# Second feed-forward layer of a fused attention and two-layer kernel: token operands spread over five pairs of chunks, swish reordered, six output buffers, right-hand pools shifted by 96 bytes

## The chip, the cores and the metric

The kernel runs on one core of a Trainium2 chip as one program. The metric is the device time of one execution in microseconds (us). One execution was also profiled; its span runs from the first to the last instruction. PE is the matmul engine (TensorE), PEld its weight loads, DVE is VectorE, ACT is ScalarE, SP issues the DMAs. Nothing runs on the host.

## The reference

Windowed attention, a gated feed-forward layer (512 to 1536 to 512) and a second feed-forward layer (512 to 2048 to 512) over 2304 tokens, all in float32. The change sits in the second layer; its arithmetic is

```python
def _moe2_ref(x, w_in, w_out):          # x 2304x512, w_in 512x2048, w_out 2048x512
    h = x @ w_in
    relu6 = np.clip(h + 3.0, 0.0, 6.0)
    g = h * relu6 / 6.0                 # called swish below
    return (g @ w_out).astype(np.float32)

def reference(**kwargs):
    ...
    attn_out = _attn_ref(**attn_kwargs)
    x = np.ascontiguousarray(attn_out.transpose(0, 2, 1, 3)).reshape(B * S, H * D)
    x = _moe_ref(x=x, **moe_kwargs)     # silu(x @ w_gate) * (x @ w_val) @ w_out
    return _moe2_ref(x=x, **moe2_kwargs)
```

## The kernel before

**Number format.** Every float32 operand of a layer matmul is split into a rounded part (hi, a cast on ACT) and the rest (lo, a subtraction on DVE). A product of two operands is three matmuls: hi by hi, lo by hi, hi by lo. So each operand costs one ACT cast and one DVE subtraction.

**First layer.** Five blocks of tokens (four of 512, one of 256) by twelve chunks of 128 hidden columns. Per chunk there are 36 matmuls: gate and value (L398 to L400, twelve each) and the way back (L451 to L453, twelve). Each chunk has three weight tiles, 36 in all. The weights are stationary operands here. They lie in two pools: `wp` on the left (`RING` = 18 buffers: tiles 0 to 16 and 35) and `wq` on the right (tiles 17 to 34, that is chunks 6 to 11 apart from the very last tile, and the way back of chunk 5). Right-hand pools are stacked downwards from the end of the memory. In the built program the tiles of `wp` start at byte 10,880 + 4096 k, a multiple of 64, and those of `wq` at 155,616 + 4096 k, 32 more than a multiple of 64. The other right-hand pools (`cv`: weights being converted; `at`: attention) have the same odd 32. Attention and the conversion of the weights run beside the first four blocks. In the last block, as chunks of `wp` fall free, it becomes a ring for the weights of the second layer.

**Second layer.** Three stages of 768 tokens, two halves of 384 each (`TH`). The hidden columns are taken as eight pairs of chunks per stage, so 24 passes of `unit`, plus one that only finishes the last. The first product of the layer is computed as a 2 by 2 block product with seven products in place of eight. Its token side needs seven operands per stage: `x11`, `x21`, `x22` and the sums `t1` to `t4`. Function `operands` makes them: 7 casts (L481), 7 subtractions for lo (L483) and 4 for the sums (L488), each 128x768. It is a generator; `advance` takes steps from it. Stage 0's operands are made during the last block of the first layer. Those of stages 1 and 2 are made during passes 5 and 6 of the stage before, six steps in the middle and six at the end of a pass.

A pass issues on PE, in this order: product `x11` (1), product `t2` (2), way back of block 11 of the pass before (9 matmuls), products `x21` (3) and `t3` (4), way back 22, products `t1` (5) and `t4` (6), way back 21, product `x22` (7), way back 12. A product is 6 matmuls of 384 columns (L518 to L520), a way back 9 of 512 (L557 to L559). Products write to two PSUM banks, `g` and `v`, in turn, so each waits until the product two before it was read: 3 waits for the copy `q1` on ACT (L582), 4 for `u2`, 5 for `h11`, 6 for `u3`, 7 for `h22` and `u4`, the next pass's 1 for `h21` and its 2 for `h12` (all L576 on DVE). The swish of a block is `swish_a` (L528, L529 on DVE and the cast `gh`, L533, on ACT) and `swish_b` (`gl`, L539 on DVE). Blocks 21 and 12 get their swish in the pass after. The tile that holds `h21` shares its buffer with the `gh` of the same block of the pass before (one tag), and so does `h12`: `h21` waits for way back 21 to have read it and `h12` for way back 12.

The order on each engine is as written from block 2 of the first layer on (`manual_schedule`); before that a scheduler sets it. All DMAs are issued on SP's queue in the order written. Pass 24 has only the four ways back; each of the last two leaves three result banks, which ACT scales into one of two buffers (L562) and SP stores (L564).

Of the kernel before, what the change touches and what calls it, by code (L numbers as in the profile page):

```python
# [21 lines left out]
NT = B * S  # L22
# [13 lines left out]
NU = NC2 // 2  # L36
RING = 3 * NC1 // 2
GB = 4
# [18 lines left out]
def attention_two_ffn(ctx: ExitStack, tc, qk, v, w, out):  # L57
# [3 lines left out]
    xp = ctx.enter_context(tc.tile_pool(name="xp", bufs=1))  # L61
    wp = ctx.enter_context(tc.tile_pool(name="wp", bufs=RING))
    early = ExitStack()
    wq = early.enter_context(tc.tile_pool(name="wq", bufs=3 * NC1 - RING, side="right"))
# [128 lines left out]
    def load_x2(s, k, j):  # L193

        t = ring_tile(("x", s, k, j), [128, 2, TH], F32, "xb")
        t0 = (2 * s + j) * TH
        lo = t0
        while lo < t0 + TH:
            tb = lo // TB
            hi = min(t0 + TH, tb * TB + SIZE[tb])  # L200
            nc.sync.dma_start(
                out=t[:, :, lo - t0:hi - t0],
                in_=x2_d[tb][:, 2 * k:2 * k + 2, lo - tb * TB:hi - tb * TB],
            )
            lo = hi
        x_raw[s, k, j] = t

    def load_ring():

        while ring_free() and (x_wanted or w_next[0] < NS * 6 * NU):  # L210
            if x_wanted:
                load_x2(*x_wanted.pop(0))
                continue
# [261 lines left out]
    def operands(s, pool):  # L475


        def split(name, t):
            hi = pool.tile([128, 2, TH], F32R, tag=f"h{name}", name="xh")
            lo = pool.tile([128, 2, TH], F32R, tag=f"l{name}", name="xl")  # L480
            nc.scalar.copy(hi, t)  # L481
            yield
            nc.vector.tensor_tensor(out=lo, in0=t, in1=hi.bitcast(F32), op=ALU.subtract)  # L483
            yield
            xops[s, name] = (hi, lo)

        def minus(out, a, b):
            nc.vector.tensor_tensor(out=out, in0=a, in1=b, op=ALU.subtract)  # L488

        x11, x12, x21, x22 = (x_raw.pop((s, k, j)) for k in range(2) for j in range(2))  # L490
        yield from split("x11", x11)
        minus(x11, x12, x11)
        yield
        yield from split("t1", x11)
        minus(x11, x22, x11)
        yield
        yield from split("t2", x11)
        yield from split("x21", x21)
        minus(x12, x22, x12)
        yield  # L500
        yield from split("t3", x12)
        minus(x21, x21, x11)
        yield
        yield from split("t4", x21)
        yield from split("x22", x22)
        for k in range(2):
            for j in range(2):
                read.add(("x", s, k, j))

# [32 lines left out]
    def ffn2_out(name, i, evac=False):  # L542
# [11 lines left out]
        for t in range(3):  # L554
# [5 lines left out]
            if end:  # L560
                ob = up.tile([128, DM], F32, tag="uh", name="ob")
                nc.scalar.activation(ob, a, AF.Copy, scale=1.0 / 6.0)  # L562
                r0 = (2 * s + j) * TH + t * 128
                nc.sync.dma_start(out=out[r0:r0 + 128, :], in_=ob)  # L564

    def unit(i, before, others):
# [7 lines left out]
        def plus(tag, a, b):  # L574
            t = fp.tile([128, TH], F32, tag=tag, name=tag)
            nc.vector.tensor_tensor(out=t, in0=a, in1=b, op=ALU.add)  # L576
            return t

        if now:
            p = product(wa, 0, x["x11"])  # L580
            q1 = fp.tile([128, TH], F32, tag="q1", name="q1")
            nc.scalar.copy(q1, p)  # L582
            p = product(w12, 1, x["t2"])
            u2 = plus("u2", q1, p)
        if before:
            before()
        ffn2_out("11", i - 1)
        if i:
            swish_a("21", i - 1, h_old.pop("21"))
        if now:  # L590
# [4 lines left out]
        ffn2_out("22", i - 1)  # L595
        if i:
            swish_b("21", i - 1)
            swish_a("12", i - 1, h_old.pop("12"))
        if now:
            swish_a("11", i, h11)  # L600
        if i:
            swish_b("12", i - 1)
        if now:
            swish_b("11", i)
        advance(others, 6)
        if now:
            p5 = product(w12, 0, x["t1"])
            h22 = plus("h22", u3, p5)
            u4 = plus("u4", u2, p5)
            p = product(wb, 1, x["t4"])  # L610
            h_old["21"] = plus("h21", u3, p)
        ffn2_out("21", i - 1)
        if now:
            p = product(w34, 1, x["x22"])
            swish_a("22", i, h22)
            h_old["12"] = plus("h12", u4, p)
            swish_b("22", i)
        ffn2_out("12", i - 1)
        advance(others, 6)
        if now:  # L620
# [15 lines left out]
    with ExitStack() as fixed:  # L636
# [7 lines left out]
        for n, (t, c) in enumerate(steps1):  # L644
            if (t, c) == (2, 0):
                fixed.enter_context(tc.manual_schedule())
            if t == NTB - 1:
                if c == 0:
# [5 lines left out]
                    prep = operands(0, xo[0])  # L654
                    x_wanted.extend((0, k, j) for k in range(2) for j in range(2))
                if c >= 2:
                    load_ring()
                if c >= 4:
                    advance(prep, 3)
            pumps = CONVERT_FIRST if t == 0 else CONVERT_NEXT  # L660
# [107 lines left out]
```

## Time and profile before

| | |
|---|---|
| three runs, median (lowest to highest) | 982.61 us (982.34 to 985.35) |
| the profiled execution: its own time | 983.48 us |
| its span | 981.6 us |
| granted clock of PE, mean (1.0 is full) | 0.982 |
| busy: PE, DVE, ACT | 933.8 us (95%), 655.3 us (67%), 380.4 us (39%) |
| first layer's last products to the end of the second layer | about 571 to 981.6 us |

How to read it: PE is busy nearly all the time, so what counts is where it waits, how fast its clock is and how long one matmul follows another. A matmul's shown duration runs past the start of the next one, since they are pipelined; the rate is read from start to start. The engine named behind an arrow is the one that ended an idle time.

### The profile page before, as it was taken

The page shows a single profiled execution, that of the slowest core. Times are in us where ns is not written, and L with a number is a line of the kernel's source. Part 1 is how long each engine was busy: PE and PEld are TensorE (multiplying, and loading weights), DVE is VectorE, ACT ScalarE, POOL GpSimd, SP SyncE. Part 2 cuts the span into 40 slices and gives each one's busy share as a digit, 9 for nine tenths or more (in the row PEclk, how much of TensorE's full clock was granted, in tenths as well). Part 3 has the DMA queues.
Part 4 walks back from the last instruction along what each step waited for, and adds up shares of the span by engine and source line. Part 5 has one row for each costly group of instructions (what it writes and reads, how often), then busy time and mean ns, then how long its engine had stood idle before and what let it go on. Part 6 is the DMA issues. An engine that isn't in the chain of part 4 may idle for free.

```text
span 981.6 us, 13330 instructions
## 1 busy us (share of the span) xinstructions
PE 933.8 (95%) x4752; PEld 805.1 (82%) x4752; DVE 655.3 (67%) x1534; ACT 380.4 (39%) x876; POOL 2.2 (0%) x12
## 2 busy tenths in 40 slices
PE   6798999999999999999999999988999988999997
PEld 6676886788888888878879998977889977998996
DVE  6899999868857676667434645566555566565554
ACT  6777776545444444444322311112121122221112
POOL 0000000000000000000000000000000000000000
PEclk9799999999999999999999999998999999999999
DMA  8455655556716554463205456555566646486501
GB/s 298 136 179 200 200 204 177 203 197 221 236 36 221 189 164 153 134 233 126 104 25 200 186 185 245 171 193 190 197 255 211 202 147 236 150 303 232 172 1 65
DMA packets 56466, 176.12 MB, mean 179 GB/s; under 512 B 5968, under 2 KB 11088, under 8 KB 55888
## 3 DMA queue, kind: packets, MB, share of 16 engines
q1 hardware_dynamic: 56400, 175.27, 51.7%
q8 instruction: 38, 0.62, 0.3%
q14 instruction: 28, 0.23, 0.1%
HBM read 140.64 MB, written 34.60 MB: 179 GB/s over the span
## 4 chain that ended last, share of the span: by engine, by line
PE 71%; DVE 15%; DMA 8%; ACT 4%; issue 2%; SPq 0%; ACTq 0%; DVEq 0%
PE acc L558 4%; PE acc L559 4%; PE acc L557 4%; PE v L400 3%; PE v L398 3%; PE v L399 3%; PE g L398 3%; PE g L399 3%; PE g L400 3%; PE acc L453 3%; PE acc L452 3%; PE acc L451 3%; DMA raw<-w_t 3%; PE g L518 3%; PE v L518 3%; PE g L520 3%
## 5 line engine op out<-in xcount | busy, mean ns | idle before, releaser
L533 ACT CAST gh<-g 128x384 fp32r<-128x384 f32 x96 | 49.3, 513 | 240.7 <-DVE g L529 240.7
L398 PE MATMUL g<-xh,wt 128*128 128x512 f32 (+1 forms) x240 | 92.4, 385 | 4.6 <-DVE u L434 2.0
L398 PE MATMUL v<-xh,wt 128*128 128x512 f32 (+1 forms) x240 | 91.0, 379 | 1.8 <-DVE u L441 1.7
L399 PE MATMUL g<-xl,wt 128*128 128x512 f32 (+1 forms) x240 | 90.0, 375 | 0.6 <-DVE xl L242 0.6
L400 PE MATMUL g<-xh,wt 128*128 128x512 f32 (+1 forms) x240 | 90.2, 376 | 0.0
L400 PE MATMUL v<-xh,wt 128*128 128x512 f32 (+1 forms) x240 | 90.1, 375 | 0.0
L452 PE MATMUL acc<-ul,wt 128*128 128x512 f32 (+1 forms) x240 | 89.6, 373 | 0.4 <-DVE ul L426 0.4
L399 PE MATMUL v<-xl,wt 128*128 128x512 f32 (+1 forms) x240 | 89.3, 372 | 0.0
L453 PE MATMUL acc<-uh,wt 128*128 128x512 f32 (+1 forms) x240 | 89.2, 372 | 0.0
L451 PE MATMUL acc<-uh,wt 128*128 128x512 f32 (+1 forms) x240 | 83.0, 373 | 2.1 <-ACT uh L421 2.1
L559 PE MATMUL acc<-wt,gl 128*128 128x512 f32 x192 | 76.9, 401 | 0.0
L558 PE MATMUL acc<-wt,gh 128*128 128x512 f32 x192 | 76.8, 400 | 0.0
L557 PE MATMUL acc<-wt,gh 128*128 128x512 f32 x192 | 75.6, 394 | 0.0
L312 ACT ACTIVATE y<-y,s 128x128 f32<-128x128 f32 x144 | 56.1, 392 | 26.1 <-DVE s L306 25.9
L518 PE MATMUL g<-xh,wt 128*128 128x384 f32 x168 | 57.7, 344 | 8.8 <-DVE u L576 7.8
L421 ACT CAST uh<-u 128x512 fp32r<-128x512 f32 (+1 forms) x60 | 34.6, 577 | 78.4 <-DVE u L441 78.4
L518 PE MATMUL v<-xh,wt 128*128 128x384 f32 x168 | 57.3, 341 | 7.4 <-DVE u L576 7.4
L434 DVE SCALAR_TENSOR_TENSOR u<-u,g 128x512 f32<-128x512 f32 (+1 forms) x60 | 37.9, 631 | 35.9 <-ACT u L433 35.4
L112 ACT ACTIVATE raw<-raw 128x512 int32<-128x512 uint32 x68 | 46.0, 676 | 37.9 <-DMA raw<-w_t 35.7
L520 PE MATMUL g<-xh,wt 128*128 128x384 f32 x168 | 57.4, 342 | 0.0
L539 DVE TENSOR_TENSOR gl<-g,gh 128x384 fp32r<-128x384 f32 x96 | 53.1, 553 | 6.1 <-ACT gh L533 6.1
L520 PE MATMUL v<-xh,wt 128*128 128x384 f32 x168 | 57.2, 341 | 0.0
(112 smaller groups left out, 2072.8 us busy)
## 6 DMA issues: line engine op xcount, KB each, us to landing
wt<-w2d SPq DMA_DIRECT2D x144, 512.0 KB, 4.6
raw<-w_t SPq DMA_DIRECT2D x68, 512.0 KB, 3.7
w2d<-ws SPq DMA_DIRECT2D x48, 512.0 KB, 3.5
qk<-qk_t SPq DMA_DIRECT2D x36, 416.0 KB, 4.2
v<-v_t SPq DMA_DIRECT2D x36, 256.0 KB, 3.8
x_out<-ob SPq DMA_DIRECT2D x18, 256.0 KB, 2.0
x2d<-xr SPq DMA_DIRECT2D x4, 1024.0 KB, 5.0
xb<-x2d SPq DMA_DIRECT2D x6, 384.0 KB, 4.3
```

The lines of the kernel that those rows point to most:

```text
L312: nc.scalar.activation(y[:, u, :], y[:, u, :], AF.Exp, bias=nm[:, 0, u:u + 1], scale=-1.0, accum_out=nm[:, 1, u:u + 1],)
L398: nc.tensor.matmul(dst, wt[:, 0, col], hi, start=kc == 0, stop=False)
L399: nc.tensor.matmul(dst, wt[:, 0, col], lo, start=False, stop=False)
L400: nc.tensor.matmul(dst, wt[:, 1, col], hi, start=False, stop=kc == KC - 1)
L451: nc.tensor.matmul(a, wt[:, 0, col], hi, start=c == 0, stop=False)
L452: nc.tensor.matmul(a, wt[:, 0, col], lo, start=False, stop=False)
L453: nc.tensor.matmul(a, wt[:, 1, col], hi, start=False, stop=c == NC1 - 1)
L518: nc.tensor.matmul(dst, wt[:, 0, col], hi[:, k, :], start=k == 0, stop=False)
L520: nc.tensor.matmul(dst, wt[:, 1, col], hi[:, k, :], start=False, stop=k == 1)
L557: nc.tensor.matmul(a, hi[:, row], wt[:, 0, :], start=begin, stop=False)
L558: nc.tensor.matmul(a, hi[:, row], wt[:, 1, :], start=False, stop=False)
L559: nc.tensor.matmul(a, lo[:, row], wt[:, 0, :], start=False, stop=end)
```

## The change

- `operands`: the same 7 casts and 11 subtractions per stage in another order, with one DVE instruction between two `yield`s (the first step has two casts and one subtraction). `advance` now takes one step at three places of a pass: before product 3's reader, between the two halves of swish 11, and between the two halves of swish 22. Passes 2 to 6 of a stage take them, so its 11 steps end in pass 5. In the last block of the first layer two steps per chunk are taken in place of three.
- The token tiles of stages 1 and 2 are loaded at pass 1 into four tiles of their own in `fp`, no longer through the ring. The ring has 15 buffers in place of 18, and `wq` 21 in place of 18.
- `swish_a` of blocks 21 and 12 stands at the start of the pass, ahead of product 1 and of `q1`; their `swish_b` stands between `q1` and `u2`. `swish_b` of 22 now stands before `h12`.
- The results go through six buffers (those of the first layer's token operands) in place of two. `store_out` issues them at the ways back, three at a time; in the last stage every second one is scaled on DVE in place of ACT.
- A tile of 24 floats (96 bytes) at the right end. All right-hand pools move down; in the built program `wq` starts at 143,232 + 4096 k, a multiple of 64, and so do `cv` and `at`.

```diff
-RING = 3 * NC1 // 2
+RING = 15
...
+    end = ctx.enter_context(tc.tile_pool(name="end", bufs=1, side="right"))
+    end.tile([128, 24], F32, name="pad")
...
-        t = ring_tile(("x", s, k, j), [128, 2, TH], F32, "xb")
+        if s == 0:
+            t = ring_tile(("x", s, k, j), [128, 2, TH], F32, "xb")
+        else:
+            t = fp.tile([128, 2, TH], F32, tag=f"x{k}{j}", name="xb")
...
     def operands(s, pool):
...
-        yield from split("x11", x11)
+        upper("x11")
+        upper("x21")
+        lower("x11")
+        yield
         minus(x11, x12, x11)
-        yield
-        yield from split("t1", x11)
+        upper("t1")
+        yield
+        lower("x21")
+        yield
+        lower("t1")
+        yield
         minus(x11, x22, x11)
-        yield
-        yield from split("t2", x11)
-        yield from split("x21", x21)
+        upper("t2")
+        yield
+        minus(x21, x21, x11)
+        upper("x22")
+        yield
+        lower("t2")
+        upper("t4")
+        yield
+        lower("x22")
+        yield
         minus(x12, x22, x12)
-        yield
-        yield from split("t3", x12)
-        minus(x21, x21, x11)
-        yield
-        yield from split("t4", x21)
-        yield from split("x22", x22)
...
+        upper("t3")
+        yield
+        lower("t4")
+        yield
+        lower("t3")
...
+    def store_out(k):
+
+        for a, r0 in done[:k]:
+            n = r0 // 128 % 6
+            ob = up.tile([128, DM], F32, tag=f"x{'hl'[n % 2]}{n // 2}", name="ob", bufs=1)
+            if n % 2 and r0 >= NT - 2 * TH:
+                nc.vector.tensor_scalar(ob, a, 1.0 / 6.0, None, op0=ALU.mult)
+            else:
                 nc.scalar.activation(ob, a, AF.Copy, scale=1.0 / 6.0)
...
     def unit(i, before, others):
...
+        if i:
+            swish_a("21", i - 1, h_old.pop("21"))
+            swish_a("12", i - 1, h_old.pop("12"))
         if now:
             p = product(wa, 0, x["x11"])
             q1 = fp.tile([128, TH], F32, tag="q1", name="q1")
             nc.scalar.copy(q1, p)
+        if i:
+            swish_b("21", i - 1)
+            swish_b("12", i - 1)
+        if now:
             p = product(w12, 1, x["t2"])
             u2 = plus("u2", q1, p)
+        store_out(3)
...
         ffn2_out("11", i - 1)
-        if i:
-            swish_a("21", i - 1, h_old.pop("21"))
+        advance(others, 1)
...
         ffn2_out("22", i - 1)
-        if i:
-            swish_b("21", i - 1)
-            swish_a("12", i - 1, h_old.pop("12"))
         if now:
             swish_a("11", i, h11)
-        if i:
-            swish_b("12", i - 1)
-        if now:
+            advance(others, 1)
             swish_b("11", i)
-        advance(others, 6)
...
             swish_a("22", i, h22)
+            advance(others, 1)
+            swish_b("22", i)
             h_old["12"] = plus("h12", u4, p)
-            swish_b("22", i)
+        store_out(3)
         ffn2_out("12", i - 1)
-        advance(others, 6)
+        if not now:
+            store_out(3)
...
-                    advance(prep, 3)
+                    advance(prep, 2)
...
-            if n == 4 and s + 1 < NS:
-                x_wanted.extend((s + 1, k, j) for k in range(2) for j in range(2))
+            if n == 1 and s + 1 < NS:
+                for k in range(2):
+                    for j in range(2):
+                        load_x2(s + 1, k, j)
...
-                prep if n in (5, 6) else iter(()),
+                prep if 2 <= n < 7 else iter(()),
```

The order on PE is the same instruction for instruction. What moves is on DVE, ACT and SP. DVE, pass 5 of stage 0 before, around `h22` and `u4` (the last two rows), which product 7 waits for; `xl` and `xb` are the operands' subtractions:

```order
L539 TENSOR_TENSOR gl<-g,gh 128x384
L528 TENSOR_SCALAR g<-h_6036 128x384
L529 SCALAR_TENSOR_TENSOR g<-g,h_6036 128x384
L528 TENSOR_SCALAR g<-h_6100 128x384
L529 SCALAR_TENSOR_TENSOR g<-g,h_6100 128x384
L539 TENSOR_TENSOR gl<-g,gh 128x384 x2
L483 TENSOR_TENSOR xl<-xb,xh 128x768
L488 TENSOR_TENSOR xb<-xb 128x768
L483 TENSOR_TENSOR xl<-xb,xh 128x768
L488 TENSOR_TENSOR xb<-xb 128x768
L576 TENSOR_TENSOR h_6153<-u_6109,v 128x384
L576 TENSOR_TENSOR u_6155<-u_6077,v 128x384
```

Four subtractions of the operands stand between product 5 and its readers. DVE now, the same stretch of a pass that makes operands (pass 4), on to the pass's end:

```order
L612 TENSOR_TENSOR u_6006<-u_5975,v 128x384
L553 TENSOR_SCALAR g<-h_5997 128x384
L554 SCALAR_TENSOR_TENSOR g<-g,h_5997 128x384
L495 TENSOR_TENSOR xl<-xb,xh 128x768
L564 TENSOR_TENSOR gl<-g,gh 128x384
L612 TENSOR_TENSOR h_6033<-u_6006,g 128x384
L612 TENSOR_TENSOR u_6035<-u_5975,g 128x384
L612 TENSOR_TENSOR h_6044<-u_6006,v 128x384
L553 TENSOR_SCALAR g<-h_6033 128x384
L554 SCALAR_TENSOR_TENSOR g<-g,h_6033 128x384
L501 TENSOR_TENSOR xb<-xb 128x768
L564 TENSOR_TENSOR gl<-g,gh 128x384
```

One subtraction stands at each place, and the swish of blocks 21 and 12 is gone from here. DVE at the change from pass 4 to 5 of stage 0, where no operands are made yet, before: `h12` of the old pass (first row), then `gl` of block 22, then `u2` of the new pass:

```order
L576 TENSOR_TENSOR h_6036<-u_6004,g 128x384
L539 TENSOR_TENSOR gl<-g,gh 128x384
L576 TENSOR_TENSOR u_6077<-q_6068,g 128x384
L528 TENSOR_SCALAR g<-h_6013 128x384
L529 SCALAR_TENSOR_TENSOR g<-g,h_6013 128x384
L576 TENSOR_TENSOR h_6100<-q_6068,v 128x384
```

And now, from pass 5 to 6, where no operands are made any more; `h12` is the second row and `u2` the next to last:

```order
L564 TENSOR_TENSOR gl<-g,gh 128x384
L612 TENSOR_TENSOR h_6217<-u_6183,v 128x384
L553 TENSOR_SCALAR g<-h_6192 128x384
L554 SCALAR_TENSOR_TENSOR g<-g,h_6192 128x384
L553 TENSOR_SCALAR g<-h_6217 128x384
L554 SCALAR_TENSOR_TENSOR g<-g,h_6217 128x384
L564 TENSOR_TENSOR gl<-g,gh 128x384 x2
L612 TENSOR_TENSOR u_6270<-q_6257,v 128x384
L612 TENSOR_TENSOR h_6288<-q_6257,g 128x384
```

Six instructions now stand between `h12` and `u2`, and `gl` of block 22 ahead of `h12`. On ACT the copy `q1` stood ahead of all four `gh` casts of its pass; now the casts of blocks 21 and 12 stand ahead of it.

## Rows read from the trace of the kernel before

**Rows 1.** Waits of PE from 571 us on: total us, times, longest

```profile
PE g L518 <- DVE u L576: 7.8, 3, 3.2
PE v L518 <- DVE u L576: 7.4, 2, 3.7
PE g L518 <- ACT q L582: 1.0, 2, 0.6
```

**Rows 2.** Stretches: us; busy us (instructions) by engine, granted clock, DMA share, GB/s

```profile
629.10:644.81 15.71, 15.71 (x80) 14.14 (x79) 8.99 (x20) 2.54 (x5) 0.00 (x0) 1.00 0.61 202
644.81:667.11 22.30, 18.61 (x80) 16.25 (x79) 12.84 (x24) 5.57 (x9) 0.00 (x0) 0.85 0.49 169
667.11:688.50 21.39, 17.79 (x79) 15.30 (x78) 14.91 (x27) 4.83 (x8) 0.00 (x0) 0.92 0.62 219
782.72:803.94 21.22, 17.53 (x79) 15.25 (x78) 12.73 (x24) 5.57 (x9) 0.00 (x0) 0.92 0.55 180
803.94:825.41 21.47, 17.73 (x80) 15.32 (x79) 15.01 (x27) 4.83 (x8) 0.00 (x0) 0.92 0.61 220
```

**Rows 3.** Timeline of pass 5 of stage 0: start us, us, engine, instruction

```profile
654.57 0.83 ACT L481 CAST xh<-xb 128x768 fp32r<-128x768 f32 x1
...
661.22 0.69 PE L518 MATMUL v<-xh,wt 128*128 128x384 f32 x1 [3.69 <-DVE u L576]
```

**Rows 4.** Instruction groups, whole run: busy us, mean ns of one, idle before

```profile
L529 DVE SCALAR_TENSOR_TENSOR g<-g,h 128x384 f32<-128x384 f32 x96 | 53.6, 559 | 3.3
...
L528 DVE TENSOR_SCALAR g<-h 128x384 f32<-128x384 f32 x96 | 33.9, 353 | 0.0
...
L483 DVE TENSOR_TENSOR xl<-xb,xh 128x768 fp32r<-128x768 f32 x21 | 19.6, 955 | 4.9 <-ACT xh L481 4.9
...
L459 DVE TENSOR_SCALAR xr<-acc 128x512 f32<-128x512 f32 x8 | 5.4, 686 | 0.8 <-PE acc L453 0.7
...
L533 ACT CAST gh<-g 128x384 fp32r<-128x384 f32 x96 | 49.3, 513 | 240.7 <-DVE g L529 240.7
...
L582 ACT COPY q<-g 128x384 f32<-128x384 f32 x12 | 5.8, 479 | 23.1 <-PE g L520 23.1
```

**Rows 5.** Timeline of an ordinary change of pass

```profile
644.77 0.56 DVE L576 TENSOR_TENSOR h<-u,g 128x384 f32<-128x384 f32 x1 [1.73 <-PE d L558]
644.81 0.33 PE L518 MATMUL v<-xh,wt 128*128 128x384 f32 x1
...
648.99 0.33 PE L518 MATMUL v<-xh,wt 128*128 128x384 f32 x1
```

**Rows 6.** Timeline of the change from pass 0 to pass 1

```profile
582.69 0.56 DVE L539 TENSOR_TENSOR gl<-g,gh 128x384 fp32r<-128x384 f32 x1
583.04 0.33 PE L518 MATMUL g<-xh,wt 128*128 128x384 f32 x1
```

**Rows 7.** DMA issues of the page: size and median us to landing

```profile
wt<-w2d SPq DMA_DIRECT2D x144, 512.0 KB, 4.6
```

**Rows 8.** Timeline of the end

```profile
974.70 0.39 PE L559 MATMUL d<-wt,gl 128*128 128x512 f32 x1
...
977.92 0.60 ACT L562 ACTIVATE ob<-d 128x512 f32<-128x512 f32 x1
```

**Rows 9.** Stretches of 36 matmuls each, and the second half of block 0

```profile
407.93:416.12 8.19, 8.19 (x38) 6.77 (x37) 6.35 (x12) 3.23 (x6) 0.00 (x0) 1.00 0.45 136
476.28:484.71 8.43, 8.43 (x37) 6.79 (x36) 4.54 (x9) 2.28 (x4) 0.00 (x0) 1.00 0.16 62
966.76:974.93 8.17, 8.17 (x37) 6.57 (x35) 3.77 (x8) 2.67 (x5) 0.00 (x0) 1.00 0.17 64
528.85:533.17 4.32, 4.32 (x39) 4.32 (x38) 1.27 (x4) 0.79 (x2) 0.00 (x0) 1.00 0.94 295
554.57:558.79 4.22, 4.22 (x38) 4.22 (x37) 2.69 (x5) 1.32 (x3) 0.00 (x0) 1.00 0.00 0
108.40:173.20 64.80, 61.59 (x301) 49.12 (x299) 63.14 (x154) 47.02 (x105) 0.00 (x0) 1.00 0.58 188
```

More of the change, by code (lines that the diff above doesn't have):

```diff
@@ L211, in load_ring @@
             if x_wanted:
-                load_x2(*x_wanted.pop(0))
+                load_x2(0, *x_wanted.pop(0))
                 continue
@@ L475, in operands, with upper, lower @@
     def operands(s, pool):
-        def split(name, t):
+        x11, x12, x21, x22 = (x_raw.pop((s, k, j)) for k in range(2) for j in range(2))
+        place = {"x11": x11, "x21": x21, "x22": x22, "t1": x11, "t2": x11, "t3": x12, "t4": x21}
+        def upper(name):
             hi = pool.tile([128, 2, TH], F32R, tag=f"h{name}", name="xh")
+            nc.scalar.copy(hi, place[name])
+            xops[s, name] = hi
+        def lower(name):
+            hi = xops[s, name]
             lo = pool.tile([128, 2, TH], F32R, tag=f"l{name}", name="xl")
-            nc.scalar.copy(hi, t)
-            yield
-            nc.vector.tensor_tensor(out=lo, in0=t, in1=hi.bitcast(F32), op=ALU.subtract)
-            yield
-            xops[s, name] = (hi, lo)
+            nc.vector.tensor_tensor(
+                out=lo, in0=place[name], in1=hi.bitcast(F32), op=ALU.subtract
+            )
+            xops[s, name] = hi, lo
         def minus(out, a, b):
             nc.vector.tensor_tensor(out=out, in0=a, in1=b, op=ALU.subtract)
-        x11, x12, x21, x22 = (x_raw.pop((s, k, j)) for k in range(2) for j in range(2))
-        yield from split("x11", x11)
+        upper("x11")
+        upper("x21")
+        lower("x11")
+        yield
         minus(x11, x12, x11)
+        upper("t1")
         yield
-        yield from split("t1", x11)
+        lower("x21")
+        yield
+        lower("t1")
+        yield
         minus(x11, x22, x11)
+        upper("t2")
         yield
-        yield from split("t2", x11)
-        yield from split("x21", x21)
+        minus(x21, x21, x11)
[6 more added lines that the diff above has]
+        yield
         minus(x12, x22, x12)
+        upper("t3")
         yield
-        yield from split("t3", x12)
-        minus(x21, x21, x11)
+        lower("t4")
         yield
-        yield from split("t4", x21)
-        yield from split("x22", x22)
-        for k in range(2):
-            for j in range(2):
-                read.add(("x", s, k, j))
+        lower("t3")
+        if s == 0:
+            read.update(("x", s, k, j) for k in range(2) for j in range(2))
+        yield
     banks = ["g", "v"]
@@ L560, in ffn2_out @@
             if end:
-                ob = up.tile([128, DM], F32, tag="uh", name="ob")
+                done.append((a, (2 * s + j) * TH + t * 128))
+    done = []
+    def store_out(k):
[5 more added lines that the diff above has]
+            else:
                 nc.scalar.activation(ob, a, AF.Copy, scale=1.0 / 6.0)
-                r0 = (2 * s + j) * TH + t * 128
-                nc.sync.dma_start(out=out[r0:r0 + 128, :], in_=ob)
+            nc.sync.dma_start(out=out[r0:r0 + 128, :], in_=ob)
+        del done[:k]
     def unit(i, before, others):
@@ L595, in unit @@
         ffn2_out("22", i - 1)
-        if i:
-            swish_b("21", i - 1)
-            swish_a("12", i - 1, h_old.pop("12"))
         if now:
             swish_a("11", i, h11)
-        if i:
-            swish_b("12", i - 1)
-        if now:
+            advance(others, 1)
             swish_b("11", i)
-        advance(others, 6)
-        if now:
             p5 = product(w12, 0, x["t1"])
@@ L654, in attention_two_ffn @@
                     prep = operands(0, xo[0])
-                    x_wanted.extend((0, k, j) for k in range(2) for j in range(2))
+                    x_wanted.extend((k, j) for k in range(2) for j in range(2))
                 if c >= 2:
```

## The prediction

> **What bounds the kernel now.** I read the waits of PE first, then the length of each pass of the second layer, then the timeline where a wait falls, then the spacing of matmuls. PE is what counts: from 571 us on it waits for DVE's `u` twice 3.2 and twice 3.7 us at most, 15.2 us in all with a fifth, shorter wait, and a little for ACT's `q1` [rows 1]. The long ones fall in passes 5 and 6 of stages 0 and 1. An ordinary pass takes 15.71 us with PE busy throughout; those four take 22.30, 21.39, 21.22 and 21.47 us [rows 2]. The excess is 86.38 - 4 x 15.71 = 23.5 us. [...] The timeline shows what stands in the way [rows 3]: ACT starts the first operand cast at 654.57, then two casts and four subtractions of 128x768 go by turns, and `h22` and `u4`, which product 7 needs, only come behind them; PE starts at 661.22 after 3.69 us of idleness. All the instructions between are work that the next stage needs, but nobody waits for them now. Outside these passes what counts is the rate at which matmuls follow each other, and the end, where ACT empties the last banks alone.
>
> **Operands spread.** Nothing is removed: the same 7 casts and 11 subtractions per stage, three subtractions of 0.955 us [rows 4] to a pass. An ordinary pass has 8.99 us of DVE in 15.71 [rows 2]; 2.9 more leaves DVE at 11.9, so they fit on the average. They must also fit in place. Two products and one way back take 648.99 - 644.81 = 4.18 us [rows 5], so product 5 starts at 8.4 and product 7 at 12.5 us of a pass. (a) One subtraction between `u2` and `h11`: product 3 ends at about 5.2, and 0.96 + 0.55 is over before 8.4. (b) One between the halves of swish 11: even if it started as product 5 ends (9.4), 0.96 + 3 x 0.55 is over at 12.0, before product 7. (c) One between the halves of swish 22: `h21` waits for way back 21 (12.5), then 0.56 + 0.35 + 0.56 + 0.96 + 0.56 brings us to 15.5; `h12` cannot start before 15.67 anyway (it starts 0.04 us before the pass ends [rows 5]) and its reader, product 2, comes about 1 us into the next pass. So (c) has the least room, half a microsecond. With no wait left the clock stays up, since no gap of microseconds precedes it, and all four passes should come to 15.71: **-23.5 us**. If the cover fails, each subtraction shows with at most 0.96 us, 11 in each of two stages: 21 us, nearly all of the gain. I take the full gain, by the room computed; the bounds are -23.5 and -2.5. The loads of the token tiles at pass 1 come a whole pass before their first reader. The ring of 15 holds two passes of six tiles and three more, and one load lands in 4.6 us [rows 7], so the next weights have more than a pass of 15.71 us in hand: nothing, and 4.6 us once at worst.
>
> **Swish ahead of `q1`, `gl` ahead of `h12`.** Product 3 needs the bank that `q1` empties. Before, ACT copies as soon as product 1 ends. Now the copy waits behind a chain on DVE and ACT: from 644.77, `h12` 0.56, then 0.353 + 0.559 + 0.353 + 0.559, the second cast 0.513 and the copy 0.479 [rows 4, 5], together 3.38 us, that is 648.15 against product 3 at 648.99. 0.84 us of room: nothing per pass. What is queued behind the copy is product 3, then everything. Between pass 0 and 1 there are no ways back to hide behind: `gl` of block 22 starts at 582.69 and now `h12` comes after it, 582.69 + 0.56 + 0.55 = 583.8, where product 2 started at 583.04 [rows 6]: **+0.75 us**, once (0 to 1.1).
>
> **The end.** PE's last matmul ends at 974.70 + 0.39 = 975.09; ACT's last scaling ends at 977.92 + 0.60 = 978.52 [rows 8], because two buffers wait for their stores. With six buffers and two engines the last bank is scaled on DVE at once: 0.686 us for 128x512 out of PSUM [rows 4], 975.8. **-2.7 us**; what follows, the last store and the closing, stays. Bounds: -1.5, if the stores, now closer together, hold each other up, and -3.2.
>
> **The right-hand pools.** The first layer has a step that no engine's wait shows. A chunk's 36 matmuls take 8.19 us when the stationary tiles come from `wp` and 8.43 us when they come from `wq` [rows 9], 227.5 against 234.2 ns from start to start. (The count in a row includes matmuls that overlap its edges.) It is not the place in memory: in pass 24 the stationary operands lie where `wq` lay, but on multiples of 64, and 36 matmuls take 8.17 us. So I put it down to the odd 32 bytes, which the pad takes away. Six chunks of `wq` in a block gain 6 x 0.24 = 1.44 us. In block 3's second half no attention runs: 1.44. In blocks 1 and 2 attention's matmuls break into half of these chunks; I take 1.0 each, of 0 to 1.44. In block 0 DVE is busy 63.14 of 64.80 us, so it is the bound there: 0, of 0 to 1.44. In the last block, 256 columns, it is the reverse: 4.32 us from `wp`, 4.22 from `wq` [rows 9]; six chunks lose 0.6. Sum **-2.8 us**, bounds -5.2 and +1.0 (if the odd 32 is not the cause: three more tiles, 36 matmuls, go right, times four blocks times 6.7 ns).
>
> [...]
>
> **Sum.** -23.5 + 0.75 - 2.7 - 2.8 = -28.3 us. The profiled execution took 983.48 us with a span of 981.6; it would take 955.2. It lies 0.87 above the median of the runs, so for a median I say 954.3, on its own 952 to 957.
>
> **Rivals.** (1) *The pad does not change the spacing.* For it: the last block shows the opposite sign, which a slower access would not. Against: pass 24's 8.17 us. Then +1.0 in place of -2.8: 954.3 + 3.8 = 958.1. (2) *The spread operands still reach PE*, through place (c) with its half microsecond. Half of each subtraction in two stages, 22 x 0.48 = 10.5: 964.8. Against it: room at each place; for it: in rows 1 ACT's `q1`, late behind operand casts, already cost PE 1.0 us. (3) *Slower: the copy `q1` becomes the bound.* Each of 23 passes hands over through seven instructions on two engines. Hand-overs cost something that I set at nothing. The change is a loss once product 3 is late by 28.3 / 23 = 1.23 us in every pass, so when the chain takes 0.84 + 1.23 = 2.07 more than 3.38 us, 0.3 us a link. At 0.35 a link the lateness is 1.6 us and the time 954.3 + 23 x 1.6 = 991. Against it: in rows 5 DVE's `h12` starts 0.04 us before PE's next product, so an engine that was let go by another does not start late by 0.3 us there. (4) *More than I take:* block 0 and attention gain too, 951.
>
> [...]
>
> **How the numbers follow.** Forecast 0.66, (1) 0.18, (2) 0.08, (3) 0.04, (4) 0.04. The range 950 to 961 holds the forecast, (1), (4); (2) and (3) are left out with 0.12. 0.3% of 982.61 is 2.9 us, about what can be told from no change. Of the cases only (3) is slower: 0.04. A mixture of small losses that comes to within 2.9 us I give 0.01. Faster: 0.95.
>
> **What would show it.** In the changed profile: passes 5 and 6 of stages 0 and 1, and passes 2 to 4, at 15.7 us with a granted clock of 1.00 and no wait of PE above 1 us from 583 us on. A wait of PE for `h12` of some 0.7 us at 583 us. In an ordinary pass the copy `q1` starts about 2.8 us after product 1 and PE does not wait for it. Chunks 6 to 11 of block 3 at 8.19 us. About 3.9 us between PE's last matmul and the span's end (6.5 before). I am wrong if PE waits for `q` or `u` in every pass, or if the four passes stay above 17 us.

## The result, and the profile after

The changed kernel took 955.57 us (median of four runs, 954.09 to 957.64) against 983.24 (982.34 to 985.35) for the kernel before in the same number of runs: a ratio of 0.9717, with a 95% interval from 0.9692 to 0.9742. The forecast was 954.3. The profiled execution took 955.52 us with a span of 953.7, against 983.48 and 981.6.

The waits of PE from 565 us on come first (total us, times, longest); they answer to [rows 1].

```profile
PE g L543 <- DVE u L612: 1.5, 1, 1.5
PE g L543 <- DVE h L612: 0.6, 1, 0.6
```

Nothing is left but the stall in pass 0 that was there before, and one new wait for `h12`. The stretches of pass 1, then passes 5, 6 and 7 of stage 0 and passes 5 and 6 of stage 1 of the changed kernel answer to [rows 2] and have the same columns:

```profile
579.44:595.97 16.53, 15.98 (x79) 14.11 (x79) 9.76 (x22) 2.95 (x6) 0.00 (x0) 1.00 1.01 390
643.09:658.80 15.71, 15.71 (x79) 14.14 (x78) 10.81 (x22) 2.43 (x5) 0.00 (x0) 1.00 0.61 204
658.80:674.51 15.71, 15.71 (x80) 14.14 (x78) 9.16 (x20) 2.43 (x5) 0.00 (x0) 1.00 0.60 202
674.51:690.21 15.70, 15.70 (x79) 14.14 (x78) 9.16 (x20) 2.43 (x5) 0.00 (x0) 1.00 0.62 200
768.75:784.45 15.70, 15.70 (x79) 14.14 (x78) 10.80 (x22) 2.43 (x5) 0.00 (x0) 1.00 0.59 198
784.45:800.16 15.71, 15.71 (x79) 14.14 (x78) 9.17 (x20) 2.44 (x5) 0.00 (x0) 1.00 0.59 198
```

The four long passes have the length of any other, PE is busy throughout, and the granted clock is 1.00. The copy `q1` starts 2.8 us after product 1, as forecast, and is not waited for; in the timeline of the changed kernel from 658.77 on, `h12`, the copy and then `u2` which reads it are

```profile
658.77 0.56 DVE L612 TENSOR_TENSOR h<-u,v 128x384 f32<-128x384 f32 x1 [0.52 <-PE d L583]
...
661.58 0.47 ACT L621 COPY q<-g 128x384 f32<-128x384 f32 x1
...
662.18 0.55 DVE L612 TENSOR_TENSOR u<-q,v 128x384 f32<-128x384 f32 x1
```

The copy ends 3.28 us after `h12` starts (3.38 had been worked out), and product 3 starts 0.9 us later. At the end of the changed kernel, which answers to [rows 8], DVE scales the last bank as soon as it is done:

```profile
949.45 0.39 PE L584 MATMUL d<-wt,gl 128*128 128x512 f32 x1
949.88 0.69 DVE L596 TENSOR_SCALAR ob<-d 128x512 f32<-128x512 f32 x1 [0.67 <-PE d L584]
```

From PE's last matmul (949.84) to the span's end it is 3.85 us; before, it was 6.55. By terms, worked out from the starts of the passes and blocks in the two traces:

| term | forecast, us | measured, us |
|---|---|---|
| passes 5 and 6 of stages 0 and 1 | -23.5 | 62.82 - 86.38 = -23.56 |
| pass 1 | +0.75 | 16.53 - 15.69 = +0.84 |
| the end | -2.7 | 3.85 - 6.55 = -2.70 |
| all before the second layer (pools) | -2.8 | 568.93 - 571.47 = -2.54 |
| sum | -28.3 | -27.96 |

The row before the sum is a difference of two single executions, like the others, and it holds more than the pools; the experiments come back to it. Of the chunks 6 to 11 of block 3, for which 8.19 us was forecast, 7, 10 and 11 take 8.16; 6, 8 and 9 take 9.20, 8.85 and 8.29.

### The profile page after: what moved, and what is told of

It is laid out like the page before. It is cut to its first block, busy times and chain, and to the rows that moved or that the text cites. A ratio compares the mean times of both kernels' runs of the same rounds, so it can differ in the third digit from the quotient of the medians.

```text
span 953.7 us, 13369 instructions
## 1 busy us (share of the span) xinstructions
PE 921.1 (97%) x4752; PEld 800.5 (84%) x4752; DVE 659.4 (69%) x1537; ACT 375.8 (39%) x873; POOL 2.2 (0%) x12
## 4 chain that ended last, share of the span: by engine, by line
PE 79%; DVE 10%; DMA 6%; ACT 4%; issue 1%; SPq 0%; ACTq 0%; DVEq 0%
PE acc L583 5%; PE acc L584 5%; PE acc L582 5%; PE v L404 4%; PE v L405 4%; PE v L406 4%; PE g L406 4%; PE g L405 4%; PE g L404 4%; PE acc L457 4%; PE acc L459 4%; PE acc L458 4%; DMA raw<-w_t 3%; PE g L543 3%; PE v L545 3%; PE g L545 3%
## 5 line engine op out<-in xcount | busy, mean ns | idle before, releaser
L404 PEld LDWEIGHTS g<-xh,wt 128*128 128x128 f32 x240 | 45.5, 190 | 15.8 <-DVE u L440 3.9
L545 PE MATMUL v<-xh,wt 128*128 128x384 f32 x168 | 56.9, 338 | 0.0
```

The source lines that it names most:

```text
L404: nc.tensor.matmul(dst, wt[:, 0, col], hi, start=kc == 0, stop=False)
L545: nc.tensor.matmul(dst, wt[:, 1, col], hi[:, k, :], start=False, stop=k == 1)
```

## The experiments

Each was an edit of the changed kernel unless it says otherwise. Their ratios are to runs of the kernel before on the same chip; its medians there lie between 983.1 and 984.0 us. The diffs are shortened, with comments added.

**The spacing of matmuls alone.** A kernel with nothing but series of matmuls, in two versions. The core of the second:

```
SERIES = [(n, so) for n in (512, 384, 256) for so in (*range(0, 128, 8), 4, 68)]
for cols, so in SERIES:
    for n in range(24):
        a = so // 4 + n % 16 * 128
        nc.tensor.matmul(banks[n // 3 % 4][:, :cols], still[:, a:a + 128], move[:, :cols], ...)
```

> Leaves the whole computation out and stores zeros: only series of 24 fp32r matmuls, 128x128 stationary, of 512, 384 and 256 columns, with the stationary tiles' start and the moving tile's start at 0, 16, 32, 48, 64 or 96 bytes past a multiple of 128; then 12 matmuls of 384 columns and 9 of 512 by turns. Theory A (where the stationary tile starts sets the spacing): 512 columns 227 ns at 0 and 64, 234 ns at 32 and 96; 256 columns 120 ns at 0 and 117 ns at 32; the moving tile's start changes nothing. Rival B (the start of the stationary tile is not the cause; what differs between the pools is something else, such as the load beside it): the same spacing at every start, to within 1 ns. Rival C (the moving tile's start): 234 where the moving tile starts at 32. For 384 columns no kernel shows a tile at 32: A says only that 0 gives 173 to 178 ns as in the second layer.

> Leaves the whole computation out and stores zeros: series of 24 fp32r matmuls of 512, 384 and 256 columns, the moving tile at a multiple of 128, the stationary tiles 0 to 120 bytes past one in steps of 8 (and 4, 68); then 12 matmuls of 384 columns and 9 of 512 by turns with four starts of either. Theory A2 (after the first series: what counts is the distance of the two starts modulo 128): 512 columns 227 ns at distance 0 alone and 233 to 234 ns elsewhere; 256 columns 113 ns at 64 alone or in a stretch around it, 116 to 120 elsewhere; 384 columns 173 ns nearly everywhere. Rival (only some starts, such as multiples of 32, behave so): the steps between show values outside 227 to 234 and 113 to 120. By turns: 4.17 to 4.21 us for 21 matmuls, as in the first series, whatever the starts.

Stretches of 24 matmuls of the first version: 512 columns with both tiles at a multiple of 128, with the stationary tiles 32 bytes on, and with the moving tile 32 bytes on:

```profile
19.19:24.64 5.45, 5.45 (x26) 4.51 (x25) 0.00 (x0) 0.00 (x0) 0.00 (x0) 1.00 0.00 0
24.64:30.23 5.59, 5.59 (x25) 4.51 (x24) 0.00 (x0) 0.00 (x0) 0.00 (x0) 1.00 0.01 3
30.23:35.83 5.60, 5.60 (x25) 4.50 (x24) 0.00 (x0) 0.00 (x0) 0.00 (x0) 1.00 0.00 0
```

From start to start (mean of a series without its first seven) that is 226.6, 233.4 and 233.4 ns. With both tiles at 32 it is 226.9 again, with the stationary tiles at 64 it is 233.5. So in these series of 512 columns the spacing goes not with where one operand starts but with how far apart the two start, and 64 bytes apart are not the same as 0 (233.5 against 226.6). Distances up to 120 bytes were tried, so no run shows the "modulo 128" of the expectations as a period. In the changed kernel the tiles of `wp` and `wq` start 256 bytes apart modulo 512 and run at the same rate (8.16 us a chunk from either): there 256 bytes made no difference. The second version, for 13 of its 18 distances in bytes, mean ns:

```
distance  0     8     16    24    32    40    48    64    80    88    96    112   120
512     226.6 230.6 233.3 230.0 233.4 233.2 233.3 233.5 232.0 233.4 234.5 233.4 226.7
384     173.4 173.4 173.4 176.8 173.3 180.0 173.3 173.4 175.9 173.3 173.4 173.4 173.4
256     119.8 115.6 118.2 122.2 118.5 119.4 118.4 113.4 118.7 113.4 117.5 120.1 119.6
```

512 columns are fast at 0 (226.6) and at 120 (226.7) only. 384 columns take 173.3 to 173.4 at most distances, but 180.0 at 40. 256 columns take 119.8 at 0, 122.2 at 24, and least, 113.4, at 64 and 88. The distance alone doesn't settle the shorter two: at 256 columns 96 bytes gave 120.0 in the first version and 117.5 here, at 384 columns 16 bytes gave 176.7 and 173.4. By turns, 21 matmuls took 4.15 to 4.22 us in all 16 combinations of starts, around the 4.18 us of the second layer [rows 5]: it has little to gain from this.

**Other pads, and the pad alone.**

```diff
-    end.tile([128, 24], F32, name="pad")
+    end.tile([128, 16], F32, name="pad")    # e2: 64 bytes; e3: [128, 8], 32 bytes
```

> The changed kernel with a pad of 64 in place of 96 bytes: the right pools still move, but keep the odd 32 bytes. Theory A (start modulo 64): chunks of wq go back to 234 ns a matmul (36 in 8.43 us), the last block's to 117; blocks 1 to 3 lose 2.9 us, three more tiles 0.6, the last block gains 0.6; the clock's fall at 176 us is gone, as in the kernel before: about 958.5 us, +2.9. Rival B (the place in memory or the smaller ring gave it): 955.6, no change, chunks at 8.17 us.

> The changed kernel with a pad of 32 in place of 96 bytes: the right pools start at multiples of 64, but 64 past a multiple of 128. Theory A (start modulo 64): as the changed kernel, 955.6 within 0.7 us, chunks of wq at 8.17 us. Rival D (start modulo 128): half or all of the gain goes, 957 to 958.5, chunks of wq at 8.3 to 8.43 us.

> The kernel before with the 96-byte pad alone. Theory A: the pad's own share, -2.5 us as its blocks showed in the changed kernel (blocks 1, 2, 3: -0.5, -1.5, -0.9; last block +0.56): 980.5 for 983.2, and a fall of the clock near 176 us in block 1, because PE, faster in block 0, waits longer for ACT's first cast there. Rival B (the pad does nothing by itself): 983.2, and no fall near 176 us.

Chunk 7 of block 3, 36 matmuls from `wq`, with the pad of 64 and with that of 32:

```profile
476.50:484.93 8.43, 8.43 (x38) 6.77 (x37) 4.58 (x9) 2.29 (x4) 0.00 (x0) 1.00 0.15 62
```

```profile
478.10:486.50 8.40, 8.40 (x37) 6.73 (x36) 4.55 (x9) 2.29 (x4) 0.00 (x0) 1.00 0.16 62
```

In the changed kernel that chunk takes 8.16 us:

```profile
474.17:482.33 8.16, 8.16 (x38) 6.76 (x36) 4.55 (x9) 2.28 (x4) 0.00 (x0) 1.00 0.16 64
```

Lengths of the first layer's blocks, from the starts of their first matmuls, us:

```
                        block 1   2       3       last    time, us  ratio to before (95%)
before                  116.5   118.1   111.0   52.6    983.24
changed (pad of 96)     116.2   116.5   110.1   53.1    955.57   0.9717 (0.9692 to 0.9742)
e2, pad of 64           116.5   117.8   111.2   52.7    958.41   0.9752 (0.9735 to 0.9769)
e3, pad of 32           116.4   117.7   111.0   52.6    958.86   0.9755 (0.9734 to 0.9776)
e4, before and the pad  114.7   116.5   109.9   53.1    981.18   0.9979 (0.9965 to 0.9993)
```

A pad of 64 moves the pools as far as matters and brings nothing: the place and the smaller ring are not the cause. A pad of 32 makes the starts multiples of 64 and brings nothing either: theory A as written (modulo 64) fell, rival D held (its time lies just above D's range). The intervals of e2 and e3 overlap that of the changed kernel, so it is the traces that show it: blocks 1 to the last together take 397.7 to 398.3 us in the three executions without the pad of 96 (before, e2, e3), and 394.2 to 396.0 in the seven with it and an unchanged last block (changed, e4, e6 to e9, e12). Block 0 takes anything from 130.9 to 134.2 us, whatever the pad. Alone, the pad saves about 2 us (0.7 to 3.4). The fall of the clock that I expected at 176 us did not come there in e4 but at 88 and 156 us; more on it below.

**Operands bundled again.** The old order and places of `operands`, all else as changed:

```diff
-        advance(others, 1)          # at the three places, passes 2 to 6
+        advance(others, 6)          # in the middle and at the end, passes 5 and 6
```

> The changed kernel with the operands made as before, six steps in the middle and six at the end of passes 5 and 6, in the old order; all else as changed. Theory A (the spreading is what saved the stalls): passes 5 and 6 of stages 0 and 1 back at 21 to 22 us, each with 3.2 to 3.7 us of idle PE and a stretch at half clock: +23.5, 979. Rival E (the earlier swish of blocks 21 and 12 and the earlier loads had already made the room): one swish pair less stands in the way, 1.5 to 2 us less per stall, and without the fall of the clock: +6 to +12, 962 to 968.

969.70 us, ratio 0.9862 (0.9845 to 0.9878): 14.1 more than the changed kernel. The waits of PE, then passes 5 and 6 of stage 0 and of stage 1:

```profile
PE v L523 <- DVE u L592: 4.7, 2, 2.4
PE g L523 <- DVE u L592: 3.7, 2, 1.8
PE g L523 <- ACT q L601: 3.1, 2, 1.6
```

```profile
641.26:659.60 18.34, 15.98 (x79) 14.05 (x78) 12.82 (x24) 5.35 (x9) 0.00 (x0) 1.00 0.56 189
659.60:680.77 21.17, 17.77 (x79) 15.34 (x78) 15.15 (x27) 4.96 (x9) 0.00 (x0) 0.92 0.47 161
775.01:793.36 18.35, 15.99 (x79) 14.06 (x78) 12.82 (x24) 5.37 (x9) 0.00 (x0) 1.00 0.57 189
793.36:812.98 19.62, 16.21 (x79) 13.95 (x78) 15.15 (x27) 4.95 (x9) 0.00 (x0) 1.00 0.49 164
```

Both theories missed. The excess over 15.71 is 14.6 us of the 23.5. With the swish of blocks 21 and 12 out of the way the long waits shrink by 1.33 us each, from 3.69 to 2.36 and from 3.18 to 1.85. The first subtraction of the operands shows why: it starts 10.63 us into pass 5 in the kernel before (first row) and 9.30 here (second row), 1.33 sooner.

```profile
655.44 0.96 DVE L483 TENSOR_TENSOR xl<-xb,xh 128x768 fp32r<-128x768 f32 x1 [0.18 <-ACT xh L481]
```

```profile
650.56 0.96 DVE L489 TENSOR_TENSOR xl<-xb,xh 128x768 fp32r<-128x768 f32 x1 [0.17 <-ACT xh L487]
```

The earlier loads, the other half of rival E, have no part in it. In the kernel before the tokens had landed more than 23 us ahead of the first cast at 654.57. The rows give the count of the loads, the shortest, median and longest issue in ns, the first and last start, and the time to landing:

```profile
L201 SPq DMA_DIRECT2D xb<-x2d x6: 360/368/462, 618.8 to 626.1; - x6
DMA to landing us min/median/max: 2.6/3.3/4.8
```

`q1`, now behind two casts that wait for DVE, costs 1.56 instead of 0.5 each time, so in all PE waits only 3.2 us less than before (11.5 in place of 14.7). The other 5.7 us can be put down to the clock: by the granted clock the four passes lost 8.5 us before [rows 2] and 1.7 here. That gain is not a steady one. After 2.36 us of waiting the clock stays up (1.00 in pass 5 of both stages) where after 3.69 it fell (0.85 and 0.92 [rows 2]), but the wait of 1.85 lowered it in pass 6 of stage 0 (0.92) and the same wait in stage 1 did not (1.00).

**All three steps at place (c).**

```diff
-            advance(others, 1)      # and none at places (a) and (b)
+            advance(others, 3)
             swish_b("22", i)
```

> The changed kernel with all three operand steps of a pass between the halves of swish 22 (place c), none at the two other places. Theory A (what counts is the room at each place): of three subtractions, 2.6 us one behind the other, about one and a half fit there; h12 comes 1.4 us later and product 2 of the next pass waits for it by 0.8 us after passes 2, 3 and 4 of stages 0 and 1, and hardly after pass 5 (two steps): six waits, +4.9 us, 960.5, with the clock at full speed since no wait reaches 2 us. Rival F (what counts is DVE's mean share, 11.9 of 15.71 us): no wait of PE, 955.6 within 0.7.

967.18 us, ratio 0.9831 (0.9816 to 0.9846): 11.6 more. PE's waits, and DVE and ACT in pass 2 of stage 0 behind swish 22:

```profile
PE g L543 <- DVE h L612: 5.7, 4, 2.2
PE v L543 <- DVE h L612: 1.7, 2, 0.9
```

```profile
611.18 0.51 ACT L558 CAST gh<-g 128x384 fp32r<-128x384 f32 x1 [5.52 <-DVE g L554]
...
611.60 1.57 ACT L489 CAST xh<-xb 128x768 fp32r<-128x768 f32 x2
...
612.46 0.96 DVE L495 TENSOR_TENSOR xl<-xb,xh 128x768 fp32r<-128x768 f32 x1 [1.39 <-ACT xh L489]
...
613.46 0.96 DVE L501 TENSOR_TENSOR xb<-xb 128x768 f32<-128x768 f32 x1
...
614.34 0.95 DVE L495 TENSOR_TENSOR xl<-xb,xh 128x768 fp32r<-128x768 f32 x1
```

There are the six waits of theory A, for `h12` at product 2; rival F is out. The price was missed: 11.6 us and not 4.9. The passes in which the waits fall grow by 10.6 us together, of which 7.4 are the waits. After passes 3 and 4 they are 0.86 and 0.61 us as expected. After pass 2 they are 2.2, since the first step subtracts what ACT has only begun to cast: DVE stands still for 1.39 us ahead of it. The full clock, expected "since no wait reaches 2 us", held in one stage only (0.91 and 1.00 in the rows below): after the same wait of 2.2 us it fell in stage 0 and not in stage 1, and in e6 it fell once after 1.85 us. No run shows a limit of 2 us, which was my estimate: in the changed kernel PE waited 2.57 us at 50.79, and the clock was 1.00 from 40 to 60 us. Passes 3 of stages 0 and 1:

```profile
612.83:632.59 19.76, 17.54 (x79) 15.22 (x78) 13.13 (x24) 3.60 (x7) 0.00 (x0) 0.91 0.47 159
744.59:762.80 18.21, 15.99 (x80) 14.10 (x78) 13.12 (x24) 3.60 (x7) 0.00 (x0) 1.00 0.52 169
```

**The swish in its old order**, operands spread as changed:

```diff
-        if i:                       # swish_a of 21 and 12 at the start of the pass
...
         ffn2_out("22", i - 1)
+            swish_b("21", i - 1)
+            swish_a("12", i - 1, h_old.pop("12"))
```

> The changed kernel with the swish in its old order (blocks 21 and 12 after the ways back 11 and 22, h12 ahead of gl22); the operands stay spread, one step at each place. Theory A (room at each place): place (b) is now the tightest; in the trace of the kernel before, u4 there ends at 640.5 and product 7 starts at 641.66, so one subtraction of 0.87 fits; passes 2 to 23 stay at 15.71, pass 1 goes back to 15.69: -0.84, 954.7 (or the changed kernel's time within the noise). Rival H (the swish had to move for the spreading to fit): PE waits for u4 before product 7 in passes 2 to 5 of stages 0 and 1, 0.3 to 1 us in each of seven or eight: 958 to 962.

954.37 us, ratio 0.9710 (0.9694 to 0.9726). Theory A holds: passes 2 to 23 take 15.71 us, pass 1 takes 15.68, and PE waits in the second layer only for the old stall of pass 0. The waits from 571 us on, and pass 5 of stage 0:

```profile
PE g L543 <- DVE u L612: 1.5, 1, 1.5
```

```profile
644.40:660.11 15.71, 15.71 (x80) 14.14 (x79) 10.63 (x22) 2.54 (x5) 0.00 (x0) 1.00 0.61 202
```

**The end.** ACT alone with six buffers (e8), and ACT alone with two (e12):

```diff
-            if n % 2 and r0 >= NT - 2 * TH:
-                nc.vector.tensor_scalar(ob, a, 1.0 / 6.0, None, op0=ALU.mult)
-            else:
-                nc.scalar.activation(ob, a, AF.Copy, scale=1.0 / 6.0)
+            nc.scalar.activation(ob, a, AF.Copy, scale=1.0 / 6.0)
```

```diff
-            ob = up.tile([128, DM], F32, tag=f"x{'hl'[n % 2]}{n // 2}", name="ob", bufs=1)
+            ob = up.tile([128, DM], F32, tag="uh", name="ob")     # e12 only
```

> The changed kernel with ACT scaling all results of the last stage too, through the six buffers. Theory A (the buffers are what shortened the end): a bank is finished every 0.68 us and ACT needs 0.60 for one, so ACT keeps up; from PE's last matmul to the end 3.85 us within 0.2: 955.6. Rival G (the second engine did it): ACT ends 1.5 to 2.7 us later, 957 to 958.3.

> The changed kernel with ACT alone for the results and two output buffers, as before the change; issue places and everything else as changed. Theory A (the number of buffers sets the end): from PE's last matmul to the end 6.5 us, as in the kernel before, 2.7 more than with six: 956.8 to 958.3. Rival J (the place where the results are issued did it, or the stores' own speed does): 3.8 to 4.5 us, 954 to 955.6.

e8 took 954.10 us, ratio 0.9699 (0.9684 to 0.9713), and 3.75 us from PE's last matmul to the end, 0.1 us less than with both engines. e12 took 982.22, ratio 0.9977 (0.9967 to 0.9988): all but some 2 us of the gain of the whole change is gone. The end took 6.57 us, as theory A said; with two buffers ACT waits there for a store, which with six it does not:

```profile
974.87 0.60 ACT L595 ACTIVATE ob<-c 128x512 f32<-128x512 f32 x1 [1.54 <-DMA x_out<-ob]
```

But that is 2.8 of the 28 us by which e12 is slower than e8, and neither theory had the rest. Most of it is a wait of PE; it, the two passes in which it falls, and then ACT's scalings and SP's queue around the first:

```profile
PE d L582 <- ACT ob L595: 19.2, 2, 11.9
```

```profile
704.86:735.43 30.57, 18.65 (x80) 16.56 (x78) 9.16 (x20) 4.40 (x9) 0.00 (x0) 0.78 0.78 276
845.38:870.08 24.70, 17.44 (x80) 15.36 (x79) 9.16 (x20) 4.40 (x9) 0.00 (x0) 0.86 0.81 272
```

```profile
708.05 0.61 ACT L595 ACTIVATE ob<-acc 128x512 f32<-128x512 f32 x1
709.27 0.60 ACT L595 ACTIVATE ob<-c 128x512 f32<-128x512 f32 x1 [0.61 <-DMA x_out<-ob]
723.98 0.60 ACT L595 ACTIVATE ob<-d 128x512 f32<-128x512 f32 x1 [14.10 <-DMA x_out<-ob]
```

```profile
707.42 2.99 SPq L207 DMA_DIRECT2D xb<-x2d  x6
710.51 4.36 SPq L222 DMA_DIRECT2D wt<-w2d  x6
715.00 9.93 SPq L596 DMA_DIRECT2D x_out<-ob  x3
```

At a change of stage the results of the old stage's second half are now stored in pass 1 of the new one, on SP's queue behind that pass's loads: six of tokens and six of weights at the first change, six of weights at the second. At the first change the first of these stores goes out at 715.00, its bank having been scaled by 708.66. With two buffers the third scaling needs the buffer of the first store, so it starts only at 723.98, and the new stage's way back waits for the bank: 30.57 + 24.70 - 2 x 15.71 = 23.9 us. With six buffers nobody waits.

**The last block 64 bytes on, and three edits together.** In e10 `xh`, `xl`, `uh` and `ul` of the 256-column block start 16 columns into their tiles. e11 adds `h12` ahead of `gl22` in pass 0 alone, and ACT alone at the end:

```diff
-        hi = up.tile([128, TB], F32R, tag=f"xh{kc}", name="xh", bufs=1)[:, :size]
+        hi = up.tile([128, TB], F32R, tag=f"xh{kc}", name="xh", bufs=1)[:, TB - size and 16:][:, :size]
```

> The changed kernel with the token operands of the first layer's last block (256 columns) 64 bytes further on in their tiles, so that their start is 64 bytes from that of the weights modulo 128. Theory A2 (the distance of the two starts sets the spacing): 113.4 ns a matmul in place of 120 for 432 matmuls, -2.85 us in the last block (53.1 to 50.3): 952.7 against 955.6. Rival I (the series alone showed it; beside DVE, ACT and the DMAs, or because weights of the second layer arrive too late, it doesn't come out): 0 to -1 us, or a new wait of PE for weights in the first passes.

> The changed kernel with the 64 bytes of the last block, h12 ahead of gl22 in pass 0 alone, and ACT alone at the end. Theory A2: -2.85 (last block), -0.84 (pass 1 at 15.69), -0.1 (end): -3.8, 951.8 against 955.6; in the trace pass 1 without a wait for h12. Rival: pass 1 keeps most of its 0.84 us, since the swish of block 12 and the copy q1 only come later too: 952.6.

e10 took 953.54 us, ratio 0.9697 (0.9684 to 0.9711). A chunk of its last block:

```profile
524.00:528.24 4.24, 4.24 (x39) 4.24 (x38) 1.27 (x4) 0.79 (x2) 0.00 (x0) 1.00 0.93 288
```

That is 117.8 ns a matmul, not 113.4; the block takes 52.2 in place of 53.1 us. The direction of A2 held, its size did not: -0.9 us lies in rival I's range. e3 shows the same rate: its pad puts `wq` 64 bytes off, and the chunks of `wq` in its last block take 4.24 us too. e11 took 953.51 us, ratio 0.9696 (0.9682 to 0.9710). Its pass 1 takes 15.66 us, its end 3.74, its last block 52.2, so by the traces it is 0.9 + 0.1 + 0.9 = 1.9 us faster than the changed kernel; the ratios' intervals overlap, so the timing alone does not show it.

## Why the prediction was right, and where it was not

*Operands.* The size was right, and so was the reason for it: room at each place (e7, e9), not DVE's mean share. The split was not seen. The prediction put all 23.5 us on the spreading; undoing it alone loses 14.6 (e6), because the new order of the swish lets the operands start 1.33 us sooner. Of the other 8.9 us that accounts for 3.2 in waits. The rest goes with a clock that fell in one of the four passes in place of all four, and the same wait lowered it in one stage and not in the other. The new order alone, on the kernel before, was not run. Undoing the order alone loses nothing (e9). Either edit covers part of the other's ground, and once the operands are spread the order is worth only its cost, pass 1. "Each subtraction shows with at most 0.96 us" was wrong as a bound: in e7 DVE stood still for another 1.39 us ahead of one, because its step held a cast on the other engine.

*Clock.* "The clock stays up" held in the second layer (1.00 in the four passes). That it would, "since no gap of microseconds precedes it", was my estimate: before, the clock was 0.85 to 0.92 in the passes with waits of 3.18 to 3.69 us [rows 2], in e6 it stayed at 1.00 after 2.36 us, and no run shows how long a gap it takes. The gain of 23.5 holds 14.7 us of waiting [rows 1, without the 1.5 of pass 0]; most of the rest is what the stretches at a lower clock had cost, 8.5 us by the granted clock of [rows 2]; in the kernel before, after the wait of 3.69 us, it was 0.51:

```profile
661.22:667.11 5.89, 5.89 (x16) 5.06 (x17) 1.39 (x4) 1.98 (x3) 0.00 (x0) 0.51 0.27 94
```

This part of the gain is not the same in every execution: in e4, which keeps the four stalls, the same four passes take 85.2 us in place of 86.4. So the match to 0.1 us is partly that forecast and measurement start from the same profile.

*Swish and `q1`.* +0.75 became +0.84; PE's wait for `h12` was forecast at 0.7 and is 0.55 us by the profile. From start to start it is more: product 2 starts 0.89 us after the last matmul of product 1 and 0.28 us ahead of its own second (580.31, 581.20 and 581.48), in place of some 0.17 each, about 0.8 us in all. The third rival, the only slower one, had no ground: the chain of seven ended 0.1 us sooner than worked out.

*The end.* The size was right, and of the two reasons given, six buffers and two engines, the second counts for nothing (e8). What the prediction left out is the change of stage: it moved the results' stores past the loads of pass 1 and put no price on that. Six buffers hid it; without them it costs 23.9 us (e12). The omission happened to be harmless.

*The pools.* -2.8 was forecast and -2.54 measured, but "the odd 32 bytes", a start off a multiple of 64, is not the cause. In the series the distance between the two operands' starts went with the spacing, 226.6 ns at 0 against 233.4 at 32 and 233.5 at 64; a pad of 96 bytes happens to put the tiles of `wq` at multiples of 128, as those of `wp` are, and a pad of 32 leaves them 64 bytes off (8.16 against 8.40 us a chunk). By theory A a pad of 32 would have done, and it does not. That the sums agree is in part luck. Blocks 1, 2, 3 and the last gave -0.4, -1.6, -0.9 and +0.6 against -1.0, -1.0, -1.44 and +0.6, block 0 and what stands ahead of it -0.3 against 0, and block 0 alone differs by 3.3 us among the executions. "In block 3's second half no attention runs" was misread: chunk 6 has eight matmuls of attention between its own, and PE waits for DVE behind chunk 8, 0.53 us now in place of 0.18, which takes that chunk's gain back.

*What blurred the sum.* In block 0 DVE is busy nearly throughout (63.14 of 64.80 us in its second half [rows 9]), so what PE gains there on its matmuls can be lost in waits. Its longest ones there are, for DVE's `u` 2.57 us in place of 1.39 (at 50.79 and 51.41), for ACT's `wt` 1.92 in place of 1.45 (at 152.15 and 152.81). The changed kernel's PE waits 0.79 us for ACT's first cast of block 1, where there was no wait over 0.15 us before, then for two more operands, as before, and its clock falls:

```profile
171.76:175.90 4.14, 2.30 (x8) 1.03 (x7) 2.95 (x5) 4.14 (x8) 0.00 (x0) 1.00 0.51 127
175.90:179.30 3.40, 3.40 (x10) 2.63 (x9) 3.37 (x8) 0.90 (x2) 0.00 (x0) 0.50 0.81 288
```

At a granted clock of 0.50 these 3.4 us cost 1.7. But the fall is not tied to the pad: the traces have it at 85 us in e2, at 52 and 86 in e3, at 52 and 178 in e9, and between 46 and 200 us not at all in e8 and e10. So of the few us by which runs and kernels differ here, some belong to this. What decides it in a given run is open.

## What to carry to other kernels

Price a step where it stands in its engine's queue, with the casts it waits for on other engines; a mean share says nothing. When several edits clear the same stall, take each away by itself before giving one the credit. Where stores move on a shared queue, look for what stands ahead of them, even if buffers hide it today. And when two pools feed the same matmul, compare the starts of their tiles (here 32 bytes apart took 233.4 ns a matmul of 512 columns, and 0 took 226.6).

## What the runs showed of the hardware that was not expected

- In the series alone, fp32r matmuls of 512 columns followed each other by 226.6 ns when both operands started at a multiple of 128 bytes and by 226.9 when both started 32 past one; at the other distances they took 230 to 234.5 (120 bytes apart excepted, 226.7). At 256 columns 0 was not the fast one: 119.8 there, 113.4 at 64. The same 64 bytes gave 117.8 in whole kernels (e3, e10); what makes the difference is open.
- After a wait of PE of 2.2 us the granted clock fell in one stage and not in the other of one execution (0.91 and 1.00, e7), and so it did after a wait of 1.85 us (0.92 and 1.00, e6), while two waits of 2.36 us in e6 left it at 1.00. So the length of the wait alone did not decide it.
- On DVE `h12`, shown as 0.56 us long, was followed by the next instruction after 0.47 us (658.77 and 659.24 in the changed kernel), and that one, 0.35 long, after 0.39. The chain added up from durations came out too long: 3.38 us was worked out for `q1`, and it took 3.28.
